# Start of a one-core attention and ELU kernel: one load moves from ScalarE's queue to SyncE's, one warm-up matmul goes, Exp gets its own column

## The chip, the cores and the metric

The kernel runs on one NeuronCore of a Trainium2 chip. The metric is the device time of one execution in microseconds. A profiled execution also has a span, from its first to its last instruction.

## What is computed

Attention over 4 batches x 12 heads, 448 tokens, head size 64, with scores soft-capped by tanh, and behind it a feed-forward layer with ELU over all 1792 tokens (768 to 2048 to 768). All data are float32.

```
scores = cap * tanh(scale * q @ k.T / cap)
attn = softmax(scores);  x = attn @ v
h = x @ w_in;  g = where(h > 0, h, exp(min(h, 0)) - 1);  out = g @ w_out
```

## The kernel before

Two heads make a pair, and there are 24 pairs. `Attention.run` treats them in 12 rounds of two pairs. A round has seven score tiles, called s_0 to s_6 below: s_0 holds the first 64 keys of both pairs and is made straight from the loaded q and k (`tile0`, L389, four matmuls at full float32 precision); s_1 to s_3 belong to the first pair and s_4 to s_6 to the second (`scores`, L372). Their operands are a rounded high part and the rest, made by VectorE in `prep_qk` (qkh at L364, qkl at L367), so that a score tile is three products for each of two heads. ScalarE turns each tile into a tile p_0 to p_6 by a Tanh (L405) and an Exp (L407), and TensorE multiplies these with v (L414, L427) and sums them (L458). A score tile takes a pair of PSUM banks of the tag "s", of which there are three sets; a fourth tile waits until the Exp of the first has read its own. The zero matmuls at the start ("warm") use one of the three as well.

The order on every engine is written by hand: `run` collects events with a time and sorts them, and each engine works through its own instructions in that order. Between the Exp of p_1 and the Tanh of s_2 ScalarE does one small Exp for the constant eps (`epsilon`, L663), whose input VectorE makes from cap (L660) behind the second pair's qkh and qkl.

The start is special. The first pair's q and k (raw0) and the second pair's (raw1) lie in one tile, `pre`, and each is loaded in two parts, `first` (512 columns: the first 64 keys and q) and `rest` (384 columns: the other keys). Three of these loads are issued ahead of a branch on the value of cap; the second part of raw1 is issued in the branch that is taken (`path("u")`). `prepare` writes zeros, runs matmuls on them, and lets ScalarE do an Exp, which loads its table of functions. SyncE issues nearly all other loads, in order: v of the first pair, cap, v of the second pair, then q, k and v of the next pairs.

When attention is done, the feed-forward layer runs in eight rounds of four token blocks (`Moe.run`, L231 to L233, three products for each float32 one), with weights split on the way by `Weights`.

Of the kernel before, what the change touches and what calls it, by code (L numbers as in the profile page):

```python
# [7 lines left out]
F32 = mybir.dt.float32  # L8
# [3 lines left out]
AF = mybir.ActivationFunctionType  # L12
# [5 lines left out]
P = 128  # L18
BANK = 512
# [20 lines left out]
def pieces(b):  # L40

    out = []
    for t, (t0, n) in enumerate(BLOCKS):
        lo, hi = max(t0, b * S), min(t0 + n, (b + 1) * S)
        if lo < hi:
            out.append((t, lo - t0, lo - b * S, hi - lo))
    return out
# [571 lines left out]
def branches(nc, pool, cap):  # L619

    one = pool.tile([1, 2], F32, name="one")
    flag = pool.tile([1, 2], I32, name="flag")
    nc.sync.dma_start(out=one[:, 0:1], in_=cap)
    yield
    a, b = one[:, 0:1], one[:, 1:2]
    nc.vector.tensor_single_scalar(out=flag[:, 1:2], in_=a, scalar=USUAL_CAP, op=ALU.is_equal)
    nc.vector.scalar_tensor_tensor(out=b, in0=a, scalar=-1.0, in1=a, op0=ALU.mult, op1=ALU.max)
    nc.vector.tensor_single_scalar(out=flag[:, 0:1], in_=b, scalar=FAST_CAP, op=ALU.is_le)
    yield flag


def prepare(nc, pool, ps):

    zero = pool.tile([P, BANK], F32, name="zero", tag="ev", bufs=2)
    nc.vector.memset(zero, 0.0)
    s = ps.tile([P, 2, BANK], F32, name="warm", tag="s", bufs=3)
    for k in range(2):
        nc.tensor.matmul(s[:, k], zero[:, :P], zero, start=True, stop=True)  # L638
    nc.scalar.activation(out=zero[:, 0:1], in_=zero[:, 0:1], func=AF.Exp)


def constants(nc, pool):
    con = Pools()
    for n in ("cap", "tsc", "eps"):
        setattr(con, n, pool.tile([P, 1], F32, name=n))
    return con


def load_cap(nc, con, cap):
    nc.sync.dma_start(out=con.cap, in_=cap.broadcast_to([P, 1]))  # L650


def scales(nc, con):
    con.tanh_scale, con.exp_scale = con.tsc[:, 0:1], con.cap[:, 0:1]
    nc.vector.reciprocal(out=con.tsc, in_=con.cap)
    nc.vector.tensor_scalar_mul(con.tsc, con.tsc, D**-0.5)
# [10 lines left out]
def attention_elu_kernel(tc, qk, v, cap, w, out):  # L667
    nc = tc.nc
    src = (qk, v)
    with ExitStack() as outer:  # L670
        cp, xp, wp, early = (
            outer.enter_context(tc.tile_pool(name=n, bufs=1)) for n in ("con", "x", "w", "early")
        )
        ps = outer.enter_context(tc.tile_pool(name="ps", bufs=1, space=PSUM))
        ask = branches(nc, cp, cap)
        next(ask)
        pre = cp.tile([P, 3 * DM], F32, name="pre")
        raw0 = pre[:, :QK]
        rawv0 = pre[:, QK : QK + NT * P].rearrange("p (t c) -> p t c", t=NT)
        raw1 = pre[:, QK + NT * P : 2 * QK + NT * P]  # L680

        first, rest = slice(0, K0 + S), slice(K0 + S, QK)
        nc.scalar.dma_start(out=raw1[:, first], in_=qk[1][:, first])
        nc.sync.dma_start(out=raw0[:, first], in_=qk[0][:, first])
        nc.sync.dma_start(out=raw0[:, rest], in_=qk[0][:, rest])
        prepare(nc, early, ps)
        flag = next(ask)
        con = constants(nc, cp)
        fast, usual = (nc.values_load(flag[0:1, k : k + 1], min_val=0, max_val=1) for k in range(2))

        def path(tag):
            general = tag == "g"
            if tag == "u":
                con.tanh_scale, con.exp_scale = D**-0.5 / USUAL_CAP, USUAL_CAP
            with ExitStack() as ctx:
                if not general:
                    ctx.enter_context(tc.manual_schedule())
                nc.scalar.dma_start(out=raw1[:, rest], in_=qk[1][:, rest])
                if tag != "u":
                    load_cap(nc, con, cap)  # L700
                    scales(nc, con)
                nc.sync.dma_start(out=rawv0, in_=v[0])
                if tag == "u":
                    load_cap(nc, con, cap)
                weights = Weights(nc, wp, pre, w)
                x = Tokens(nc, xp, early)
                moe = Moe(nc, early, ps, weights, x, out)
                with tc.tile_pool(name=f"at{tag}", bufs=1) as sb, tc.tile_pool(
                    name=f"dr{tag}", bufs=1, space=DRAM
                ) as dr:  # L710
                    if general:
                        general_attention(nc, sb, ps, x, con, src)
                        weights.scalar = True
                        for _ in range(2 * FT):
                            weights.load()
                            weights.run(WSTEPS)
                        for p in range(3 * PPB):
                            for t, *_ in pieces(p // PPB):
                                if t < 2:
                                    x.split(p, t)  # L720
                        for i, h in enumerate(moe.begin()):
                            moe.hidden(0, 0, i, h)
                            moe.elu(0, 0, i, h)
                    else:
                        Attention(nc, sb, ps, dr, x, con, src).run(weights, moe, (raw0, raw1), rawv0)
                with tc.tile_pool(name=f"late{tag}", bufs=1) as late:
                    weights.late = x.late = moe.late = late
                    weights.load(2)
                    moe.run()

        with tc.If(usual > 0) as branch:
            path("u")
        with branch.Else():
            with tc.If(fast > 0) as other:
                path("f")
            with other.Else():
                path("g")
# [45 lines left out]
```

## Time and profile before

| What | Value |
|---|---|
| Time, median of 3 runs | 635.49 us (635.42 to 635.73) |
| Profiled execution, its own time | 633.79 us |
| Its span | 631.9 us |
| Mean granted TensorE clock | 0.995 |
| Busy share of TensorE, VectorE, ScalarE | 98%, 70%, 45% |

The profiled execution is 1.70 us shorter than the median of the timed ones; 1.89 us of its time lie outside the span. Busy shares are averages over attention (until about 160 us) and the feed-forward layer, which have different limits.

### The profile page before, as it was taken

The page shows a single profiled execution, that of the slowest core. Times are in us where ns is not written, and L with a number is a line of the kernel's source. Part 1 is how long each engine was busy: PE and PEld are TensorE (multiplying, and loading weights), DVE is VectorE, ACT ScalarE, POOL GpSimd, SP SyncE. Part 2 cuts the span into 40 slices and gives each one's busy share as a digit, 9 for nine tenths or more (in the row PEclk, how much of TensorE's full clock was granted, in tenths as well). Part 3 has the DMA queues.
Part 4 walks back from the last instruction along what each step waited for, and adds up shares of the span by engine and source line. Part 5 has one row for each costly group of instructions (what it writes and reads, how often), then busy time and mean ns, then how long its engine had stood idle before and what let it go on. Part 6 is the DMA issues. An engine that isn't in the chain of part 4 may idle for free.

```text
span 631.9 us, 8710 instructions
## 1 busy us (share of the span) xinstructions
PE 620.6 (98%) x3412; PEld 462.1 (73%) x3412; DVE 444.6 (70%) x671; ACT 283.3 (45%) x399; POOL 62.3 (10%) x40
## 2 busy tenths in 40 slices
PE   6999999999999999999999999999999999999996
PEld 2444444444588888888888888888888888888885
DVE  3799899999777557675676867576767576574453
ACT  4999999999635453223222222222232123122110
POOL 0001010010011211120211112111111111110000
PEclk9999999999999999999999999999999999999999
DMA  5435556652151221120211113111111112000224
GB/s 183 142 118 173 188 154 198 184 174 64 31 159 50 66 86 50 51 100 1 101 50 51 51 50 101 50 51 51 51 51 50 51 54 97 1 2 0 101 101 155
DMA packets 26227, 54.30 MB, mean 86 GB/s; under 512 B 9538, under 2 KB 13634, under 8 KB 26178
## 3 DMA queue, kind: packets, MB, share of 16 engines
q1 hardware_dynamic: 25746, 53.07, 25.9%
q8 instruction: 29, 0.48, 0.3%
q10 hardware_dynamic: 432, 0.59, 0.3%
q14 instruction: 20, 0.16, 0.1%
HBM read 47.97 MB, written 5.59 MB: 85 GB/s over the span
## 4 chain that ended last, share of the span: by engine, by line
PE 89%; DVE 7%; DMA 1%; issue 1%; ACT 0%; POOL 0%; ACTq 0%; DVEq 0%; POOLq 0%
PE h L231 12%; PE h L232 12%; PE h L233 12%; PE o L231 12%; PE o L233 12%; PE o L232 12%; PE pv L414 7%; PE s L372 6%; DVE u L448 2%; PE sum L458 2%; PE pv L427 1%; DVE qkl L367 1%; DMA pre<-in_qk_dram 1%; PE s L389 1%; PE warm L638 1%
## 5 line engine op out<-in xcount | busy, mean ns | idle before, releaser
L231 PE MATMUL o<-gh,wh 128*128 128x512 f32 (+1 forms) x380 | 138.3, 364 | 0.2 <-ACT acc L290 0.2
L232 PE MATMUL o<-gl,wh 128*128 128x512 f32 (+1 forms) x380 | 138.2, 364 | 0.0
L233 PE MATMUL o<-gh,wl 128*128 128x512 f32 (+1 forms) x380 | 138.1, 363 | 0.0
L231 PE MATMUL h<-xh,wh 128*128 128x512 f32 x288 | 112.4, 390 | 0.1
L232 PE MATMUL h<-xl,wh 128*128 128x512 f32 x288 | 112.1, 389 | 0.0
L233 PE MATMUL h<-xh,wl 128*128 128x512 f32 x288 | 112.0, 389 | 0.0
L306 DVE TENSOR_TENSOR acc<-o,acc 128x1024 f32<-128x1024 f32 (+1 forms) x83 | 89.1, 1089 | 10.3 <-PE o L233 10.3
L254 ACT ACTIVATE gh<-e 128x512 fp32r<-128x512 f32 (+1 forms) x64 | 37.0, 579 | 103.6 <-DVE e L249 103.6
L245 ACT ACTIVATE e<-h 128x512 f32<-128x512 f32 (+1 forms) x64 | 34.6, 541 | 103.6 <-PE h L233 99.8
L231 PEld LDWEIGHTS o<-gh,wh 128*128 128x128 f32 x380 | 71.7, 189 | 12.1 <-ACT acc L290 0.6
L233 PEld LDWEIGHTS o<-gh,wl 128*128 128x128 f32 x380 | 71.7, 189 | 11.3
L232 PEld LDWEIGHTS o<-gl,wh 128*128 128x128 f32 x380 | 71.7, 189 | 11.2
L407 ACT ACTIVATE p<-s 128x896 f32<-128x896 f32 x84 | 77.2, 919 | 2.7
L405 ACT ACTIVATE s<-s 128x896 f32<-128x896 f32 x84 | 76.5, 911 | 3.8 <-PE s L389 1.6
L255 DVE TENSOR_TENSOR gl<-e,gh 128x512 fp32r<-128x512 f32 (+1 forms) x64 | 41.8, 653 | 41.3 <-ACT gh L254 40.6
L147 POOL TENSOR_TENSOR pre<-pre,wq 128x768 int32<-128x768 int32 x18 | 35.5, 1974 | 344.0 <-DVE pre L144 300.8
L246 DVE TENSOR_SCALAR e<-e 128x512 f32<-128x512 f32 (+1 forms) x64 | 26.5, 414 | 55.4 <-ACT e L245 55.2
L231 PEld LDWEIGHTS h<-xh,wh 128*128 128x128 f32 x288 | 54.1, 188 | 12.6 <-DVE e L249 0.9
L233 PEld LDWEIGHTS h<-xh,wl 128*128 128x128 f32 x288 | 54.1, 188 | 11.4
L232 PEld LDWEIGHTS h<-xl,wh 128*128 128x128 f32 x288 | 54.1, 188 | 10.9
L414 PE MATMUL pv<-p,vf 128*64 128x448 f32 x276 | 59.5, 552 | 0.1
L249 DVE SCALAR_TENSOR_TENSOR e<-h,e 128x512 f32<-128x512 f32 (+1 forms) x64 | 40.0, 625 | 2.2
(85 smaller groups left out, 725.8 us busy)
## 6 DMA issues: line engine op xcount, KB each, us to landing
pre<-in_w_dram SPq DMA_DIRECT2D x18, 768.0 KB, 4.4
wr<-in_w_dram SPq DMA_DIRECT2D x14, 768.0 KB, 4.2
raw<-in_qk_dram SPq DMA_DIRECT2D x22, 448.0 KB, 4.5
vf<-in_v_dram SPq DMA_DIRECT2D x23, 256.0 KB, 4.3
rb<-rec SPq DMA_DIRECT2D x48, 112.0 KB, 2.9
out_dram<-acc SPq DMA_DIRECT2D x9, 512.0 KB, 2.8
den<-sums SPq DMA_DIRECT2D x48, 1.8 KB, 2.1
out_dram<-acc SPq DMA_DIRECT2D x2, 256.0 KB, 3.5
```

The source lines that it names most:

```text
L147: nc.gpsimd.tensor_tensor(out=vi, in0=vi, in1=q, op=ALU.add)
L231: mm(acc, wh[:, m, :], ph, start=first, stop=False)
L232: mm(acc, wh[:, m, :], pl, start=False, stop=False)
L233: mm(acc, wl[:, m, :], ph, start=False, stop=last)
L249: nc.vector.scalar_tensor_tensor(out=ev, in0=h, scalar=0.0, in1=ev, op0=ALU.max, op1=ALU.add)
L254: nc.scalar.activation(out=gh, in_=ev, func=AF.Copy)
L255: nc.vector.tensor_tensor(out=gl, in0=ev, in1=gh.bitcast(F32), op=ALU.subtract)
L306: self.nc.vector.tensor_tensor(out=o, in0=s, in1=o, op=ALU.add)
L372: yield lambda a=a, b=b, i=i: self.nc.tensor.matmul(s, a[o, k], b[o, :S], start=i == 0, stop=i == 2)
L405: self.nc.scalar.activation(out=s, in_=s, func=AF.Tanh, scale=self.con.tanh_scale)
L407: self.nc.scalar.activation(out=pt, in_=s, func=AF.Exp, scale=self.con.exp_scale)
L414: self.nc.tensor.matmul(out[o, :S], w[j], x[j], **flags)
```

## The change

The `rest` load of the second pair is issued by SyncE as its first instruction in the branch instead of by ScalarE. One zero matmul of 512 columns is left of two. The Exp that loads the table works on a column of its own, in a second tile, which VectorE clears ahead of the zeros; before, it overwrote a column of the zeros that the matmuls read.

```diff
 def prepare(nc, pool, ps):
 
-    zero = pool.tile([P, BANK], F32, name="zero", tag="ev", bufs=2)
+    zero, one = (pool.tile([P, BANK], F32, name=f"start{i}", tag="ev", bufs=2) for i in range(2))
+    nc.vector.memset(one[:, 0:1], 0.0)
+    nc.scalar.activation(out=one[:, 0:1], in_=one[:, 0:1], func=AF.Exp)
     nc.vector.memset(zero, 0.0)
     s = ps.tile([P, 2, BANK], F32, name="warm", tag="s", bufs=3)
-    for k in range(2):
-        nc.tensor.matmul(s[:, k], zero[:, :P], zero, start=True, stop=True)
-    nc.scalar.activation(out=zero[:, 0:1], in_=zero[:, 0:1], func=AF.Exp)
+    nc.tensor.matmul(s[:, 0], zero[:, :P], zero, start=True, stop=True)
...
-                nc.scalar.dma_start(out=raw1[:, rest], in_=qk[1][:, rest])
+                nc.sync.dma_start(out=raw1[:, rest], in_=qk[1][:, rest])
```

On SyncE, at the branch, the difference reads as follows (a line in a row is that of the kernel before, `pre` is the tile with raw0, raw1 and the first v; the names behind these rows differ by their numbers alone):

```order
 L689 ISA x2
 L731 COMPARE_AND_BRANCH
+L698 DMA pre<-in_qk_dram 128x384
 L702 DMA pre<-in_v_dram 128x512
 L650 DMA cap<-in_cap_dram 128x1
```

One issue more stands ahead of the first v and of cap, and so ahead of every later load of SyncE.

On ScalarE, from the start to the first Tanh, the difference reads as follows (start_78 is the column of its own, s_0 and p_0 are the first tiles):

```order
 L683 DMA pre<-in_qk_dram 128x512
-L639 ACT_TABLE_LOAD
-L639 ACTIVATE zero<-zero 128x1
+L636 ACT_TABLE_LOAD
+L636 ACTIVATE start_78<-start_78 128x1
 L689 TENSOR_LOAD flag x2
 L731 COMPARE_AND_BRANCH
-L698 DMA pre<-in_qk_dram 128x384
-L405 ACTIVATE s_0_140<-s_0_140 128x2x448
-L407 ACTIVATE p_0_166<-s_0_140 128x896
```

Behind the branch ScalarE's next instruction is now the first Tanh; the Exp ahead of the branch stands in the same place and works on another tile.

## Rows read from the trace of the kernel before

**Rows 1.** The page: busy time by engine, and the chain that ended last by engine.

```profile
PE 620.6 (98%) x3412; PEld 462.1 (73%) x3412; DVE 444.6 (70%) x671; ACT 283.3 (45%) x399; POOL 62.3 (10%) x40
...
PE 89%; DVE 7%; DMA 1%; issue 1%; ACT 0%; POOL 0%; ACTq 0%; DVEq 0%; POOLq 0%
```

**Rows 2.** The chain of waits to 60 us: start, duration in us, what.

```profile
1.46 3.79 PE warm L638 x4
...
5.28 0.20 ACT zero L639
...
6.24 6.19 DMA pre<-in_qk_dram
...
14.23 1.00 PE s L372 x4
15.23 2.94 PE pv L414 x8
...
20.50 0.75 PE s L389 x8
...
29.02 1.66 PE pv L414 x8
```

**Rows 3.** The timeline to 30 us, all engines: start, duration in us, what, idle before.

```profile
3.68 0.33 SPq L702 DMA_DIRECT2D pre<-in_v_dram  x1
...
5.17 1.77 PE L389 MATMUL s<-pre 64*64 64x448 f32 x8
...
5.49 1.03 DVE L367 TENSOR_TENSOR qkl<-pre,qkh 128x832 fp32r<-128x832 f32 x1
...
7.12 0.90 ACT L405 ACTIVATE s<-s 128x896 f32<-128x896 f32 x1 [1.64 <-PE s L389]
...
9.81 0.92 ACT L407 ACTIVATE p<-s 128x896 f32<-128x896 f32 x1
12.53 0.59 DVE L364 CAST qkh<-pre 128x832 fp32r<-128x832 f32 x1 [6.01 <-DMA pre<-in_qk_dram]
13.15 1.02 DVE L367 TENSOR_TENSOR qkl<-pre,qkh 128x832 fp32r<-128x832 f32 x1
...
14.28 0.20 ACT L663 ACTIVATE eps<-eps 128x1 f32<-128x1 f32 x1 [3.55 <-DVE eps L660]
...
14.39 0.90 ACT L405 ACTIVATE s<-s 128x896 f32<-128x896 f32 x1
...
15.32 0.92 ACT L407 ACTIVATE p<-s 128x896 f32<-128x896 f32 x1
...
18.84 0.92 ACT L407 ACTIVATE p<-s 128x896 f32<-128x896 f32 x1
```

**Rows 4.** DMA issues by form: issuer, KB each, median us from issue to landing.

```profile
pre<-in_qk_dram SPq DMA_DIRECT2D x1, 256.0 KB, 2.9
pre<-in_v_dram SPq DMA_DIRECT2D x1, 256.0 KB, 2.7
...
pre<-in_qk_dram ACTq DMA_DIRECT2D x1, 192.0 KB, 6.2
...
cap<-in_cap_dram SPq DMA_DIRECT2D x1, 0.5 KB, 3.5
```

**Rows 5.** DMA queues from 6 to 10 us: packets, MB, share (q1: SyncE, q10: ScalarE).

```profile
DMA packets 545, 1.08 MB, mean 271 GB/s; under 512 B 112, under 2 KB 112, under 8 KB 545
...
q1 hardware_dynamic: 545, 1.08, 77.5%
```

**Rows 6.** The same from 10 to 12.5 us.

```profile
q10 hardware_dynamic: 144, 0.20, 21.2%
```

**Rows 7.** Line L389 in the whole span: duration in ns (min/median/max), first and last start.

```profile
L389 PE MATMUL s<-raw x88: 536/536/536, 20.3 to 147.0; 64*64 64x448 f32 x88
L389 PEldq EVENT_SEMAPHORE  x12: 51/51/51, 4.1 to 144.4; - x12
...
L389 PE MATMUL s<-pre x8: 951/978/1006, 5.2 to 6.0; 64*64 64x448 f32 x8
```

**Rows 8.** Busy time by stretch: PE, PEld, DVE, ACT, POOL, granted clock, DMA share, GB/s.

```profile
9.90:13.30 3.40, 0.04 (x4) 0.07 (x2) 0.74 (x2) 0.83 (x1) 0.00 (x0) 1.00 0.64 249
...
14.20:17.70 3.50, 3.47 (x12) 1.11 (x12) 3.15 (x6) 3.35 (x5) 0.00 (x0) 0.53 0.00 0
...
30.00:115.00 85.00, 85.00 (x628) 37.31 (x624) 80.20 (x114) 82.83 (x96) 5.09 (x2) 1.00 0.55 167
```

**Rows 9.** Waits of ScalarE from 14 to 162 us: total, times, longest.

```profile
ACT s L405 <- PE s L372: 1.3, 3, 0.8
```

## Prediction

> **What bounds the kernel now.** I read the page first: TensorE is busy 98% of the span and carries 89% of the chain that ended last [rows 1]. So a microsecond counts only where TensorE stands still or is slowed. The table of stretches shows where: from 30 to 115 us it is busy 85.00 of 85.00 us, but from 9.9 to 13.3 us it works 0.04 of 3.40, and from 14.2 to 17.7 us its granted clock is 0.53 [rows 8]. The chain of waits tells what the start hangs on: the zero matmuls, the small Exp behind them, the issue of the second pair's rest load at 6.24, its 6.19 us to landing, and then work on what it brought [rows 2]. The timeline names who waits for that load: VectorE's qkh at 12.53 (6.01 us idle, released by the DMA), then qkl, then eps, and ScalarE's eps at 14.28 after 3.55 us idle [rows 3]. ScalarE does its list in order, so the Tanh of s_2 at 14.39 waits behind eps, though s_2 was long there. From 14.23 on the chain is work.
>
> **The rest load.** SyncE's first issue in the branch is at 3.68, the first v [rows 3]; it lands 2.7 us later [rows 4]. The rest load takes its place, is smaller (192 KB against 256 KB), and by that row lands at about 6.4. VectorE is busy with the first pair's qkl until 5.49 + 1.03 = 6.52 [rows 3], so qkh starts at about 6.55, and eps is ready for ScalarE as much later as it was after qkh before, 14.28 - 12.53 = 1.75 us: at 8.3. ScalarE wants it only after the Exp of p_1, which ended at 9.81 + 0.92 = 10.73 and will end a little earlier (next step). So the 3.55 us of idle time go, and the load has over a microsecond to spare: only a landing after about 7.9 would cost something, then one for one.
>
> Why did the load take 6.2 us before? Between 6 and 10 us SyncE's queue moved 545 packets and ScalarE's none, though its load was issued at 6.24 [rows 2, 5]; all 144 packets of it came after 10 [rows 6]. It waited behind what SyncE had issued. In front of it on SyncE there is only the first pair's. The Trainium skill (DMA: Bandwidth & Descriptors, "Issuing engines are not separate DMA queues") says that DMAs of several engines end up on the same 16 DMA engines and interleave, and that another issuer saves only issue time; by that rule moving the load gains its earlier issue, 2.56 us, and no more. The trace does not show the interleaving in that stretch. What 6.2 us would cost at the new place is a rival below.
>
> **SyncE's other loads** go out some 0.4 us later (3.68 to the next issue). The first v landed at 6.4, and TensorE wants it after the Exp of p_1, near 10; cap landed about 3.5 us after its issue, some 7.6 by an issue at about 4.05, so 8.0 now, and VectorE wants it at 8.2, ScalarE at 9.8. ScalarE loses one issue of about 0.35 us that lay in its idle 1.64 us. I cost these at nothing; if cap came after 9.8, its delay would be paid in full.
>
> **One matmul on zeros instead of two.** The four halves took 3.79 us, from 1.46 to 5.25 [rows 2]. Half of them end at about 3.4 (the clear of the column puts them off by some 0.1 us, as small VectorE operations take here; nothing waits for that). tile0 started at 5.17, just as the zeros ended, while the semaphore for its data had been passed at 4.1 (landing 1.16 + 2.9 = 4.06) [rows 3, 4, 7]. So the zeros held it back and the data takes over: start at about 4.2, 0.97 earlier. It still runs at half speed: its matmuls took 978 ns against 536 ns in later rounds [rows 7], and I keep 1.77 us. The first Tanh then starts at 7.12 - 0.97 = 6.15; ScalarE is there, for its Exp no longer waits for the matmuls (5.28 before, about 2.6 now). The next three activations follow on ScalarE's own pace, since s_1 (its second product needs qkl at 6.52) is done by about 7.6 and its Tanh is due at 7.9. The Exp of p_1 ends at 9.76, eps follows in the pipeline, and the Tanh of s_2 starts at 9.76 instead of 14.39: **4.63 us earlier**. If tile0 does not move, it is 14.39 - 10.73 = 3.66.
>
> **What becomes of TensorE's lead.** In the stretch at 0.53 the two products of p_1 and p_2 with v took 2.94 us, against 1.66 in the next round [rows 2]: 1.28 lost. If TensorE does not stand still for 3.4 us, I expect it to keep the full level there. It can't use all of this: tile0 of the second round needs the banks that the Exp of p_4 frees. Before, that Exp ended at 18.84 + 0.92 = 19.76 and tile0 began at 20.50 [rows 2, 3], 0.74 late for lack of TensorE time. At full clock TensorE is there first and starts 0.03 after it, so **0.71 us more**, making 5.34 at this point. From there TensorE has work without a pause, as before. Is ScalarE able to follow? Its pace is faster: in the whole of attention it waited for scores three times, 1.3 us in all [rows 9], and it worked 82.83 of 85 us [rows 8]; it starts 0.71 less early than TensorE and makes that up. VectorE has 4.8 us to spare in the same 85. Later loads are issued when buffers come free, so they move along. I carry the 5.34 us to the end whole.
>
> The sum against the profiled execution: 633.79 - 4.63 - 0.71 = 628.45. Against the median, 1.70 us above it, the same saving gives 635.49 - 5.34 = 630.15, and that is the forecast, about 0.84% less.
>
> **Rivals.**
>
> *Clock late.* With less work on TensorE and a pause from 3.4 to 4.2, the lower level may last longer. Half speed costs little while TensorE waits for ScalarE anyway: at 1.00 us for four score matmuls [rows 2], six take at most 1.5, and s_1 to s_3 are done by 11, s_4 not being allowed before 9.76. I estimate that each microsecond at the low level after about 10.5 costs 1.28 / 2.94 = 0.44. If the clock rose only at 17.7, as it did in the trace after its fall, 7.2 x 0.44 = 3.1 us would go: gain 2.2, 633.3. For it: the trace gives no rise without the second matmul. Against it: after the standstill before 13.3, which was four times this pause, the clock was up again some 4 us after work had resumed, and here that would be at about 8. The Trainium skill (TensorE: Matmul & The Clock Gate, "Part 1") says that the throttled level is the default and that activity releases it. By that rule taking away warm-up speaks against this change; the row of tile0 at half speed agrees with the default, and no row shows when the release comes now.
>
> *Load as slow as before.* If the rest load took 6.2 us from 3.68, it would land at 9.87, the Tanh of s_2 would start 14.39 - 12.43 = 1.96 later, at 11.83, and the gain would be 2.56 + 0.71 = 3.3: 632.2. Against it: the first v's row in that place.
>
> *Tile0 not earlier.* If something other than the zeros held it, the branch for one, the gain is 3.66 + 0.71 = 4.4: 631.1. For it: the start so close on the end of the zeros can be chance; against it, the semaphore passed at 4.1.
>
> *No change.* The move does not do what it says if the load still lands at 12.4, behind the loads that SyncE issues after it; then ScalarE's eps stands where it was, and the time with it: 635.5. Rows 5 show such an overtaking between two queues, none within one.
>
> *Slower.* The low clock is the only mechanism that I find for it: at 0.44 a microsecond it eats the 5.34 us if it lasts 12.1 us past 10.5. From 22.6 us on the kernel is slower; with TensorE at half clock until 26 it ends at 637.0. The busy rows make this unlikely, as TensorE has hardly a pause after 4.2.
>
> **How the numbers follow.** Forecast as summed (gain 5.0 to 5.6) 0.60; clock late 0.13; load slow 0.08; tile0 not earlier 0.09; no change 0.05; slower 0.05. A measurement of this kernel can tell about 0.2%, 1.3 us, from no change. The first four lie beyond it: faster 0.90, same 0.05, slower 0.05. The range reaches up to the slow load and tile0 cases, 632.3, and leaves out most of the late clock, no change and slower; down to 629.0, for the whole 1.28 us of slowed work instead of 0.71 (0.6 more) and for the timed runs, whose 1.70 us above the profile I can't place.
>
> **What would show it.** Right: the rest load lands near 6.4 and VectorE's second qkh starts at 6.5 to 7; tile0 at 4.2; ScalarE without a pause behind the Exp of p_1 and the Tanh of s_2 at 9.8; granted clock 1.00 from 10 on and no stretch near 0.5; tile0 of the second round at about 15.2; and from there every row 5.3 us earlier. Wrong: matmuls of s_4 or p_1 at 900 ns, eps waiting for cap or the load, or a lead at 20 us that is smaller at 160 us.

## The result and the profile after

| | Before | Changed |
|---|---|---|
| Median | 635.73 us (635.42 to 636.22, 6 runs) | 629.69 us (629.47 to 629.86, 6 runs) |
| Profiled execution | 633.79 us | 629.86 us |
| Span | 631.9 us | 627.6 us |

The ratio is 0.9905, 95% interval [0.9892, 0.9917]: 5.3 to 6.9 us less. The forecast was 630.2 us (629.0 to 632.3), a saving of 5.34; the medians differ by 6.04, the profiled executions by only 3.93. Both differences are taken up below.

The chain of waits of the changed kernel, from the first load to the second round (start, duration in us, what):

```profile
1.16 2.97 DMA pre<-in_qk_dram
...
4.26 1.84 PE s L389 x8
...
6.19 0.91 ACT s L405
...
9.79 0.09 ACT eps L663
9.88 0.82 ACT s L405
...
11.69 0.97 PE pv L414 x4
...
15.24 0.96 PE s L389 x8
```

The zeros, the small Exp and the 6.19 us of the rest load [rows 2] are no longer in it. It starts with the first pair's first load, goes through tile0 and then from one activation of ScalarE to the next. The second round's tile0 starts at 15.24 instead of 20.50.

The timeline of the changed kernel, at the places that rows 3 show of before:

```profile
3.69 0.34 SPq L698 DMA_DIRECT2D pre<-in_qk_dram  x1
...
4.26 1.77 PE L389 MATMUL s<-pre 64*64 64x448 f32 x8 [0.69 <-DMA pre<-in_qk_dram]
...
6.32 0.59 DVE L364 CAST qkh<-pre 128x832 fp32r<-128x832 f32 x1
...
9.29 0.16 DVE L660 SCALAR_TENSOR_TENSOR eps<-cap 128x1 f32<-128x1 f32 x1 [1.33 <-DMA cap<-in_cap_dram]
9.69 0.19 ACT L663 ACTIVATE eps<-eps 128x1 f32<-128x1 f32 x1
9.78 0.91 ACT L405 ACTIVATE s<-s 128x896 f32<-128x896 f32 x1
```

tile0 now waits for a DMA. The second pair's qkh starts at 6.32 without a wait behind VectorE's work. ScalarE has no idle time ahead of eps. But VectorE stood 1.33 us for cap, and eps was ready only 0.24 us before ScalarE took it up.

The DMA issues of the same stretch (issuer, KB, us to landing; the row with x2 holds both rest loads, so the second pair's own is read by itself: 2.4 us):

```profile
pre<-in_qk_dram SPq DMA_DIRECT2D x2, 192.0 KB, 2.7
...
cap<-in_cap_dram SPq DMA_DIRECT2D x1, 0.5 KB, 4.7
```

Busy time by stretch after (columns as in rows 8):

```profile
9.00:12.00 3.00, 2.29 (x14) 0.88 (x14) 0.97 (x4) 2.97 (x5) 0.00 (x0) 1.00 1.02 373
12.00:15.00 3.00, 3.00 (x24) 1.18 (x20) 3.00 (x4) 2.94 (x4) 0.00 (x0) 1.00 0.21 84
```

ScalarE works 2.97 and 2.94 of 3.00 us where before it worked 0.83 of 3.40 [rows 8], and the granted clock stays at 1.00, the upper level of 2.4 GHz.

### The profile page after: what moved, and what is told of

Read it like the earlier page. It is cut to its first block, busy times and chain, and to the rows that moved or that the text cites. A ratio compares the mean times of both kernels' runs of the same rounds, so it can differ in the third digit from the quotient of the medians.

```text
span 627.6 us, 8706 instructions
## 1 busy us (share of the span) xinstructions
PE 618.4 (99%) x3410; PEld 461.6 (74%) x3410; DVE 444.4 (71%) x672; ACT 282.9 (45%) x399; POOL 62.3 (10%) x40
## 4 chain that ended last, share of the span: by engine, by line
PE 84%; DVE 9%; ACT 2%; DMA 2%; issue 1%; SPq 1%; POOL 1%; DVEq 0%; POOLq 0%; ACTq 0%
PE o L231 11%; PE o L232 11%; PE o L233 11%; PE h L231 11%; PE h L233 11%; PE h L232 11%; PE pv L414 7%; PE s L372 5%; DVE u L448 2%; PE sum L458 2%; PE pv L427 1%; PE s L389 1%; DVE xl L216 1%; DVE qkl L367 1%; DMA pre<-in_w_dram 1%
## 5 line engine op out<-in xcount | busy, mean ns | idle before, releaser
L232 PEld LDWEIGHTS h<-xl,wh 128*128 128x128 f32 x288 | 54.1, 188 | 10.9
```

What stands on the lines that cost most here:

```text
L232: mm(acc, wh[:, m, :], pl, start=False, stop=False)
```

## The experiments

The verdict of a run is its ratio to runs of the kernel before made beside it, as the median of before moved between 634.8 and 635.7 us from one set to the next. Each profiled execution has one more number that proved useful: the start of the second round's tile0 in its chain of waits. The table is in the order of that number; the fourth column is the second less the third.

| Kernel | Profiled execution, us | Second tile0 starts | Rest | Median, us | Ratio [95%] |
|---|---|---|---|---|---|
| before, again | 634.75 | 21.18 | 613.57 | 634.78 | 0.9999 [0.9990, 1.0008] |
| before | 633.79 | 20.50 | 613.29 | 635.73 | |
| rest load late | 632.71 | 18.87 | 613.84 | 632.71 | 0.9970 [0.9957, 0.9984] |
| standstill filled | 632.87 | 18.79 | 614.08 | 634.19 | 0.9992 [0.9982, 1.0003] |
| cap late | 632.66 | 18.57 | 614.09 | 633.02 | 0.9970 [0.9959, 0.9982] |
| one zero matmul only | 630.79 | 16.97 | 613.82 | 630.91 | 0.9942 [0.9923, 0.9960] |
| move only | 629.80 | 16.14 | 613.66 | 629.80 | 0.9916 [0.9903, 0.9929] |
| changed, two zeros | 630.22 | 16.14 | 614.08 | 629.97 | 0.9920 [0.9907, 0.9933] |
| first pair first | 630.02 | 16.11 | 613.91 | 630.03 | 0.9922 [0.9905, 0.9940] |
| changed, again | 629.53 | 15.68 | 613.85 | 629.27 | 0.9913 [0.9896, 0.9930] |
| column only | 630.07 | 15.61 | 614.46 | 629.94 | 0.9923 [0.9905, 0.9940] |
| no zeros | 628.85 | 15.35 | 613.50 | 629.17 | 0.9909 [0.9897, 0.9922] |
| new start only | 629.22 | 15.28 | 613.94 | 629.22 | 0.9910 [0.9896, 0.9925] |
| changed | 629.86 | 15.24 | 614.62 | 629.69 | 0.9905 [0.9892, 0.9917] |

All fourteen rests lie between 613.29 and 614.62, though the starts differ by 5.94: what the first 21 us gain or lose reaches the end within about 1.3 us, and nothing later gives it back by rule.

**The kernel before, again** (no edit).

> The kernel before, unchanged, timed against itself, because its timed runs (635.73 us) lie 1.9 us above its profiled execution (633.79 us) while those of the changed kernel (629.69) agree with its profiled execution (629.86). Theory A (the low stretch of TensorE's clock behind the standstill differs from run to run): ratio 1.000, and the spans of single runs go with their mean granted clock, longer spans at a lower clock than the 0.995 of the profiled execution, by some 1.9 us. Rival B (the difference lies outside the start, in the output or between runs): the mean clock is 0.995 in all runs, and spans differ without it.

Measured: ratio 0.9999; 633.59 to 635.99 us over 12 runs. This profiled execution had a longer fall of the clock than the first. Its stretches (columns as in rows 8):

```profile
9.90:13.30 3.40, 0.00 (x0) 0.00 (x0) 0.55 (x1) 0.40 (x1) 0.00 (x0) 0.82 0.60 236
12.00:18.70 6.70, 4.98 (x16) 1.55 (x16) 5.41 (x9) 4.13 (x6) 0.00 (x0) 0.50 0.02 7
```

The clock stood at 0.50, the lower level of 1.2 GHz, through 6.70 us instead of 3.50 with a mean of 0.53 [rows 8], and tile0 of the second round came 0.68 later. So the standstill is not worth the same in every run. The mean clock of single runs orders their times in part: of the 66 timed runs of before whose clock is on record, the 12 at 0.997 have a median of 634.2 us (632.8 to 634.8), the 45 at 0.992 or 0.993 one of 635.3 (633.3 to 636.4). It is a rough measure, as it also counts some 3 us behind the last matmul, where both traces of before show the lower level. Theory A is half right: a longer fall goes with about 1 us, and the spread at one and the same clock is larger.

**The move only.**

```diff
-                nc.scalar.dma_start(out=raw1[:, rest], in_=qk[1][:, rest])
+                nc.sync.dma_start(out=raw1[:, rest], in_=qk[1][:, rest])
```

> The load moved to SyncE, the start of before (two zero matmuls, Exp on their column). Theory A: the standstill and the fall of the clock go, but tile0 stays at 5.17, so that the Tanh of s_2 comes at 10.75: about 1.0 us above the changed kernel, 630.7. Rival B (the earlier tile0 is worth nothing, since the load or cap arrives too late for it to count): as the changed kernel, 629.7. Rival C (the zero matmuls and the column do the work): as before, 635.7.

Measured: 629.80 us (628.78 to 630.22). tile0 at 5.17 and the Tanh of s_2 at 10.69, as theory A has it, and the second tile0 0.90 later than in the changed kernel (16.14 against 15.24). The time is 0.58 us above that of the new start alone (629.22, same chip), not 1.0; by the median alone rival B's 629.7 fits better.

**The new start only** (the changed kernel with the load back on ScalarE).

```diff
-                nc.sync.dma_start(out=raw1[:, rest], in_=qk[1][:, rest])
+                nc.scalar.dma_start(out=raw1[:, rest], in_=qk[1][:, rest])
```

> The new start (one zero matmul, Exp on a column of its own), the load still issued by ScalarE. ScalarE passes the branch at about 3.4 instead of 6.2 and issues the load ahead of SyncE's first in the branch. Theory A (only who is issued first counts, not the queue): it lands at about 6.5, and the time is that of the changed kernel, 629.7 within 0.3. Rival B (ScalarE's queue is held back while SyncE's has work, as from 6 to 10 us in the trace of before): it lands after 9, the Tanh of s_2 starts at 11 or later, 631 to 633.5.

Measured: 629.22 us (628.92 to 629.27), as fast as the changed kernel (629.69, and 629.27 when it ran again). The row of its timeline that decides it:

```profile
3.08 0.34 ACTq L698 DMA_DIRECT2D pre<-in_qk_dram  x1
```

And the row of its DMA issues from 3 to 8 us:

```profile
pre<-in_qk_dram ACTq DMA_DIRECT2D x1, 192.0 KB, 3.4
```

ScalarE, no longer waiting for the zeros, issues the load at 3.08, ahead of SyncE's 3.67, and it lands at 6.5 while VectorE is still busy. Theory A holds: the move is not needed once the Exp has its own column.

**The changed kernel with two zeros.**

```diff
-    nc.tensor.matmul(s[:, 0], zero[:, :P], zero, start=True, stop=True)
+    for k in range(2):
+        nc.tensor.matmul(s[:, k], zero[:, :P], zero, start=True, stop=True)
```

> The changed kernel with two zero matmuls. Theory A: tile0 waits for their end again and starts at 5.2 instead of 4.26, all behind it 0.95 us later: 630.6. Rival B (longer work ahead of tile0 brings the clock up earlier, which pays for the wait): within 0.3 us of the changed kernel, with score matmuls at full speed from about 7.4.

Measured: 629.97 us, 0.75 above the new start alone on the same chip. tile0 starts at 5.21. Theory A by sign, with a smaller size. Rival B's clock came too (the score matmuls run at full speed from 6.8 on), but in this trace it did not pay for the wait: the second tile0 starts at 16.14.

**The column only** (before, with nothing but the Exp's own column).

```diff
-    zero = pool.tile([P, BANK], F32, name="zero", tag="ev", bufs=2)
+    zero, one = (pool.tile([P, BANK], F32, name=f"start{i}", tag="ev", bufs=2) for i in range(2))
+    nc.vector.memset(one[:, 0:1], 0.0)
+    nc.scalar.activation(out=one[:, 0:1], in_=one[:, 0:1], func=AF.Exp)
...
-    nc.scalar.activation(out=zero[:, 0:1], in_=zero[:, 0:1], func=AF.Exp)
```

> The kernel before with nothing but the column of its own for the Exp: two zero matmuls, load on ScalarE. Theory A (the load was late because ScalarE passed the branch late, so either edit alone repairs it): as with the move alone and as with two zeros and the move, 0.3 to 1.0 us above the changed kernel. Rival B (the queue matters too): 2 us or more above it.

Measured: 629.94 us, 0.67 above the changed kernel on the same chip (629.27). Either the move or the column repairs the late load. Its trace also suggests why two zeros cost less than 0.97. tile0 here, out of the timeline:

```profile
5.21 1.16 PE L389 MATMUL s<-pre 64*64 64x448 f32 x8
```

It took 1.16 us and not 1.77: with TensorE at work since 1.5, the clock can be up before tile0 is through (0.99 us in the second trace of before). So what the second zero matmul costs in waiting it can in part pay back in speed.

**One zero matmul only** (before, with one instead of two; Exp on their column, load on ScalarE).

```diff
-    for k in range(2):
-        nc.tensor.matmul(s[:, k], zero[:, :P], zero, start=True, stop=True)
+    nc.tensor.matmul(s[:, 0], zero[:, :P], zero, start=True, stop=True)
```

> The kernel before with one zero matmul instead of two, Exp still on their column, load on ScalarE. The Exp starts at 3.4 instead of 5.3, the load is issued at 4.3 to 4.4 between SyncE's cap and its second v. Theory A (loads of the two queues are served in the order of their issue): it lands at 7 to 7.9, and the time is that of the changed kernel within 0.4 us. Rival B (ScalarE's queue is served only when SyncE's is empty, as the stretch from 6 to 10 us could be read): it lands at 9 or later, and the time lies 1.5 to 4 us above the changed kernel.

Measured: 630.91 us (630.03 to 632.03), 1.64 above the changed kernel. The chain of waits shows the load and what waited:

```profile
4.54 5.02 DMA pre<-in_qk_dram
...
9.65 0.60 DVE qkh L364
...
11.41 0.20 ACT eps L662
```

Issued at 4.54, it landed at 9.56, 5.0 us later, so theory A fails: a load of ScalarE that is issued behind SyncE's v, cap and v is slow. Landing and time are rival B's, but its reason in the strict form fails too. The queues of this run from 7 to 8 us (packets, MB, share):

```profile
q1 hardware_dynamic: 68, 0.11, 46.9%
q10 hardware_dynamic: 69, 0.09, 28.7%
```

Here both queues moved, nearly packet for packet. The Tanh of s_2 came at 11.52, which is the landing plus 1.96.

**The standstill filled** (before, with four matmuls more on data that are there; nobody reads their result).

```diff
         for g in groups:
+            if (n, g) == (0, 4):
+                t = self.ps.tile([P, BANK], F32, name="fill", tag="pv1", bufs=1)
+                for _ in range(4):
+                    self.nc.tensor.matmul(t, self.raw[0][:, :P], self.raw[0][:, :BANK], start=True, stop=True)
             s = self.room(n, g)
```

> The kernel before with four extra matmuls (q and k of the first pair, 128x512, into the bank of pv1, nobody reads the result) between s_3 and s_4, so that TensorE works where it stood still from 9.9 to 13.3. Load, eps and ScalarE are late as before. Theory A (the fall of the clock has a price of its own, capped by ScalarE): the clock stays at 1.00, the eight products of p_1 and p_2 take 1.7 instead of 2.9 to 3.3, tile0 of the second round follows the Exp of p_4 at once; 0.7 to 1.4 us below the kernel before, with the spread of its runs gone. Rival B (the low stretch costs nothing, because ScalarE sets the pace in the first round): as before, and as widely spread.

Measured: 634.19 us against 634.99, ratio 0.9992 [0.9982, 1.0003], and 632.87 to 636.27 us over 11 runs. Its stretches, to be set beside those of [rows 8]:

```profile
9.90:13.30 3.40, 3.40 (x11) 1.25 (x11) 1.69 (x3) 0.19 (x2) 0.00 (x0) 1.00 0.54 213
14.20:17.70 3.50, 3.02 (x20) 1.17 (x16) 3.29 (x4) 3.44 (x5) 0.00 (x0) 1.00 0.00 0
```

TensorE is busy and the clock stays up, but ScalarE's standstill is there. In this trace the second tile0 follows the Exp of p_4 at once, as theory A says. The Tanh of s_2 out of the timeline, and tile0 out of the chain of waits:

```profile
13.34 0.90 ACT L409 ACTIVATE s<-s 128x896 f32<-128x896 f32 x1
...
18.79 0.95 PE s L389 x8
```

The second tile0 starts 1.71 us earlier than in the first trace of before (20.50). Of this 1.05 was there at the Tanh of s_2 (14.39 before), as the load was issued and landed earlier here (5.94 and 11.38); the other 0.66 is the clock. Over all runs the ratio puts the fall of the clock alone at 0.5 us and the medians at 0.8, with an interval from 1.1 us less to 0.2 more, so that zero is not excluded. And the spread did not go: runs at a mean clock of 0.997 to 0.999 lie 3.4 us apart. So most of it comes from elsewhere; see below.

**No zeros.**

```diff
-    nc.vector.memset(zero, 0.0)
-    s = ps.tile([P, 2, BANK], F32, name="warm", tag="s", bufs=3)
-    nc.tensor.matmul(s[:, 0], zero[:, :P], zero, start=True, stop=True)
```

> The changed kernel without any zero matmul. Theory A (the data set tile0's start, and half speed costs little while TensorE waits for ScalarE): tile0 at 4.1 to 4.3, the Tanh of s_2 at 9.8 to 10.1, 0 to 0.4 us above the changed kernel. Rival B (the zero matmul brings the clock up in time): score matmuls at half speed until 11 or later, p_1 and p_2 at half speed too, 1 to 3 us above it.

Measured: 629.17 us (628.85 to 629.31), no slower than the changed kernel. Theory A. tile0 at 4.23 and the Tanh of s_2 at 9.90, with the score matmuls at half speed until past 10. The one zero matmul that is left buys nothing that these runs can tell.

**Cap late** (the changed kernel, cap's load four issues later).

```diff
-                if tag == "u":
-                    load_cap(nc, con, cap)
+                con.src = cap if tag == "u" else None
...
+        if self.con.src is not None:
+            at(1.0, load_cap, self.nc, self.con, self.con.src)
```

> The changed kernel with cap's load four issues later on SyncE, behind two loads of v and one of q and k. Theory A (cap has almost no room: its eps was ready 0.2 us before ScalarE wanted it): cap lands at 11 to 12 instead of 9.2, and the delay of eps behind 9.7 is paid in full, with the fall of TensorE's clock if the standstill is long: 1.5 to 3 us above the changed kernel. Rival B (TensorE's lead over ScalarE hides it): within 0.3 us of it.

Measured: 633.02 us, ratio 0.9970. In its trace VectorE stood 3.60 us for cap, eps was at 11.76 instead of 9.69, TensorE waited 2.13 us for the Exp of p_2, the clock fell, and the second tile0 came 3.3 us later (18.57 against 15.24). Theory A, a little more than its upper end by the medians (3.3 us above 629.69, where 3 was the most expected).

**Rest load late** (the changed kernel, the load four issues later on SyncE).

```diff
-                nc.sync.dma_start(out=raw1[:, rest], in_=qk[1][:, rest])
+                def load_rest():
+                    nc.sync.dma_start(out=raw1[:, rest], in_=qk[1][:, rest])
+                con.late = load_rest
...
+        at(-1.35, self.con.late)
```

> The changed kernel with the rest load behind v, cap, v and the third pair's q and k on SyncE. Theory A (the prediction's rule: after a landing at 7.9 each microsecond costs one): it lands at 9.5 to 10.5, the Tanh of s_2 starts 1.96 later, at 11.5 to 12.5, 1.7 to 2.7 us above the changed kernel. Rival B (part of the wait is given back, as TensorE and ScalarE have slack later in the round): less than 1 us above it.

Measured: 632.71 us (631.55 to 634.85), ratio 0.9970. Issued at 5.48, the load took 5.4 us, the second pair's qkh began at 10.89 and the Tanh of s_2 at 12.76. That is 2.98 after 9.78, and the start of the second tile0 moved by 3.63. Theory A in the rule; the landing was later than I expected, and the fall of the clock comes on top: 3.0 us above 629.69, where 2.7 was the most expected.

**The changed kernel, again** (no edit).

> The changed kernel, unchanged, on one chip with the next three, as a yardstick. 629.2 to 629.9, ratio 0.990 to 0.992, its runs within 0.5 us of each other (those of before spread over 3).

Measured: 629.27 us (629.21 to 629.53), ratio 0.9913. In this trace cap was late by a hair: eps at 10.13 with 0.15 us idle ahead of it, released by VectorE.

**First pair first** (without zeros and with the rest load on ScalarE, as above; cap ahead of v; and the first loads dealt out anew).

```diff
-        nc.scalar.dma_start(out=raw1[:, first], in_=qk[1][:, first])
-        nc.sync.dma_start(out=raw0[:, first], in_=qk[0][:, first])
-        nc.sync.dma_start(out=raw0[:, rest], in_=qk[0][:, rest])
+        nc.scalar.dma_start(out=raw0[:, first], in_=qk[0][:, first])
+        nc.sync.dma_start(out=raw0[:, rest], in_=qk[0][:, rest])
+        nc.sync.dma_start(out=raw1[:, first], in_=qk[1][:, first])
```

> A version that may beat the changed kernel: no zero matmul, the second pair's rest load on ScalarE behind the branch, ScalarE's first load is now the first pair's first part, SyncE loads the first pair's rest ahead of the second pair's first part, and cap ahead of v in the branch. Theory A (the chain at the start is first loads, tile0, ScalarE): half of tile0 runs while the second pair's first part lands near 4.8, the first Tanh starts at 5.8 to 5.9 instead of 6.2, 0.2 to 0.4 us below the changed kernel. Rival B (tile0 needs both pairs, and the second pair's first part is now third in line): the first Tanh at 6.4 to 6.8, 0.2 to 0.6 us above it.

Measured: 630.03 us, 0.76 above the changed kernel. Its timeline shows rival B:

```profile
3.51 3.42 PE L389 MATMUL s<-pre 64*64 64x448 f32 x8 [3.51 <-DMA pre<-in_qk_dram]
...
5.17 0.29 PEld L389 LDWEIGHTS s<-pre 64*64 64x64 f32 x4 [1.37 <-DMA pre<-in_qk_dram]
...
7.04 0.90 ACT L405 ACTIVATE s<-s 128x896 f32<-128x896 f32 x1 [4.39 <-DVE qkh L364]
```

tile0 begins 0.75 earlier, but the second pair's first part, third in line, landed 3.5 us after its issue at 1.58. Only then, at 5.17, does tile0's second half begin, and the first Tanh is at 7.04 instead of 6.19. (Its row names VectorE's qkh as the last to signal, but this Tanh reads nothing of qkh; what it reads is tile0's result, done at 6.93.) No version here beats the changed kernel by more than the runs can tell.

## Why the prediction was right

The changed kernel with one thing undone at a time gives the steps in turn.

**The rest load was what the start waited for.** Right. Predicted: landing at about 6.4, second qkh at 6.55, no idle time of ScalarE before eps; measured 6.1, 6.32, none. The rule that a landing after 7.9 costs one for one also held: in the two traces in which the load came late, the Tanh of s_2 began about two microseconds after the landing (9.56 to 11.52, and 10.9 to 12.76). The prediction took the move for the cause. The runs show that the order of issue is the cause: with the Exp on its own column ScalarE issues the load at 3.08, and the move adds nothing that these runs can tell. The prediction had the number for it (the Exp at about 2.6; measured 2.44), but did not carry it on to the load that ScalarE issues behind that Exp.

**SyncE's other loads cost nothing.** Right in the sum, wrong in the room. I put cap's landing at 8.0 with 1.8 us to spare; it landed at 9.25, 4.7 us after its issue, with eps 0.24 us ahead of need. So one of the prediction's signs of being wrong, eps waiting for cap, came that near. When the same kernel ran again cap was 0.15 us late. The 0.4 us of the new issue ahead of it is not the whole of the difference; a small load behind two large ones took 1.2 us more than the row of before (3.5, [rows 4]).

**One zero matmul less: 0.97 us.** Right in the traces (tile0 at 4.26 for a predicted 4.2, the Tanh of s_2 at 9.78 for 9.76), too large in the medians: leaving the second zero matmul in costs 0.6 to 0.75 us (three comparisons). The step that was mis-sized is "it still runs at half speed": true behind one zero matmul (1.77 us in all six traces), but behind two tile0 took only 0.98 to 1.16 us in three of six. That this is the difference in the medians is argued; single timed runs leave no trace.

**TensorE's lead: 0.71 us.** The second tile0 started at 15.24 (predicted 15.2), 5.26 earlier than before, against 4.61 at the Tanh of s_2: 0.65 of it arrived. All fourteen traces bear the term out: from the Tanh of s_2 to the second tile0 it is 5.44 to 5.47 us in the ten in which the clock does not fall ahead of it, and 6.11 to 6.70 in the four in which it does (both of before, cap late, rest load late). Of the gain 0.21 went again at once, since a tile0 that waits for its bank takes 0.95 to 0.97 us, and one that follows on other work 0.75 [rows 2]. What it is worth at the end, in the timed runs, the filled standstill leaves open between nothing and 1.1 us.

**"Clock late" came about in part and cost nothing that these runs can tell.** The score matmuls ran at half speed until about 8.3 in one trace of the changed kernel and until about 10.6 in the other, and without any zero matmul until past 10. The changed kernel's two medians are 629.69 and 629.27 and that without zeros is 629.17, so a later rise does not go with a longer time. The prediction's reason holds that far: until about 10.5 TensorE waits for ScalarE anyway. A rise much later than that, which is what the rival priced, was not seen. The Trainium skill (TensorE: Matmul & The Clock Gate, "Part 1") has the low level as the default that work lifts; the half-speed first matmuls agree, and what the rule warns of cost nothing measurable in these first 10.6 us.

**The sum, 5.34 us, and the 3.93 and 6.04 of the two comparisons.** The rest of the profiled executions behind the second tile0 was 613.29 before and 614.62 after, the two ends of all fourteen. So these two profiles understate the gain by 1.33, and 5.26 - 1.33 = 3.93 closes. The profile shows 0.23 of it between the second tile0 and the feed-forward layer, nearly all at tile0 itself; another 0.28 lies inside the feed-forward layer (its first matmul came 5.03 earlier, its last output issue 4.75), 0.43 behind the last output issue and 0.39 outside the span. As other kernels have any value between, I take all but the first for what differs from run to run. The other way, the medians of before lie 1.0 to 1.9 us above its first profiled execution: that one was early. Its mean clock, 0.995, is also above that of 45 of the 66 timed runs (0.992 or 0.993), so a shorter fall of the clock may be part of it. Set against the four sets of before (634.8 to 635.7) and the two of the changed kernel, the saving is 5.1 to 6.5 us, and 5.34 lies in it.

**What stays open** is why the runs of before spread over 3 us. The clock is a part of it at most: with the standstill filled the runs still lie 3.4 us apart. In the three traces with its order of loads the rest load was issued at 6.24, 6.25 and 5.94 and landed at 12.43, 12.66 and 11.38, and those were the times at which everything behind it began; every kernel in which a load that is waited for came late spread over 1.9 to 3.6 us (only the first six runs of before over less, 0.8), and those in which it came early over 0.3 to 1.4. That the landing varies so from run to run is argued from this and not shown for single runs.

## What to carry to other kernels

A load that an engine issues in its own instruction order is as late as whatever that engine waits for first; look at the issue time, then at what else was issued before it, and only then at the queue. Where a start-up dummy (a table load, warm-up work) shares a buffer with another engine's dummy, the false dependency can hold up a real load. When two edits repair the same wait, their gains don't add: run each alone before keeping both.

## What the runs showed of the hardware

- A load's time to landing grew with what had been issued before it, on either queue: the same 192 KB took 2.4 to 3.4 us when issued at 3.1 to 3.7 us, ahead of the branch's other loads (on SyncE or on ScalarE), 5.0 us when issued at 4.54 behind three of SyncE's, 5.4 at 5.48 behind four on SyncE itself, and 5.4 to 6.4 at 5.94 to 6.25 behind five or six (three traces). The Trainium skill's rule (DMA: Bandwidth & Descriptors, "Issuing engines are not separate DMA queues") that loads of several engines interleave is borne out by the 68 and 69 packets from 7 to 8 us of the run with one zero matmul; in the three traces with the order of before, ScalarE's first packet moved only 3.0 to 4.0 us after the issue, against 1.0 to 1.5 in the four others in which ScalarE issued this load, and why it was so there stays open.
- cap's 0.5 KB took between 3.1 and 5.4 us to land in the fourteen traces: a small load is not a quick one.
- The same program's fall of the clock behind the same standstill lasted about 3.4 us in one trace and at least 6.7 in another.
- The granted clock reads 1.00 from the first row on, though the first matmuls take 951 to 1006 ns against 536 later [rows 7]: in the first 10 us the durations tell the level, not that column.
